# Mamba-2 scan and merged experts on one core: an earlier decay store, another load order, and new constants for the planner

## The chip, the cores and the metric

The kernel runs on one core of a Trainium2 chip. The core has five engines that run side by side, each in the order of its own instructions: TensorE (PE, with its weight loads shown as PEld), VectorE (DVE), ScalarE (ACT), GpSimd (POOL) and SyncE (SP). SP computes nothing here; it issues nearly all DMA transfers, in order. The metric is device time in microseconds, the median of several runs. Lower is better.

## The reference, cut to what matters

Two blocks follow each other. The first is a Mamba-2 scan over 4 sequences of 768 positions, with 8 heads of width 32 and a state of 16. The reference works in chunks; within a chunk:

```python
cum = np.cumsum(la, axis=-1)                    # la = log of the clipped decays a
L = np.exp(cum[:, :, :, None] - cum[:, :, None, :]) * causal
M = np.einsum('bhin,bhjn->bhij', Cc, Bc) * L
y = M @ xc + (Cc @ state) * np.exp(cum)[..., None]
state = decay_full * state + sum_j(Bc_j xc_j * decay_from_j)
```

The result, 3,072 tokens of width 256, goes through four experts, each with a hidden width of 1,024:

```python
p = domain_probs / (domain_probs.sum(-1, keepdims=True) + 1e-09)
for e in range(E):
    out += p[:, e:e + 1] * (np.maximum(x @ w1[e], 0.0) @ w2[e])
```

All of it is float32.

## The kernel before, in words

**The scan.** The sequences are cut into 24 chunks of 128 positions. The matrix L of a chunk is not made with exponentials: DVE runs a multiply-add scan over the decays (`scan`, L494), with the first decay of each head set to zero. For chunks 0 to 2 the decays are spread over the partitions by matmuls (`spread`, L618) and scanned from PSUM. From chunk 3 on (`SPREAD = 3`) they come by DMA: the cut decays `a_cut` are stored once to DRAM (`acut_d`), and `load_decays` (L438) reads a chunk's 4 KB back into all 128 partitions, 512 KB in all, into a tile `ab`. An uncut copy goes to `ac_d`; `load_heads` (L444) reads it for chunks from 4 on, and a scan at L778 makes the state's decays `dec` of it. `score` (L477) makes C times B, DVE multiplies it with L (L796, the masks `MT`), and `outputs` (L818, L510) makes a chunk's results.

**The experts.** The hidden width of an expert is cut into 4 slices of 256, so there are 16 slices. Five blocks of tokens are worked on (`ORDER = B, B, B, H, H`); a block B takes four chunks, a block H six. Within a block the products of slices and token pairs are done with fewer block products than the plain way, in the manner of Strassen: sums of weight blocks (L961), sums of token blocks (L980) and sums of results take the place of some products. A product is four matmul records at L872. A first-layer product is gated, which is ReLU times the probability, on DVE (L907); sums of gated values (L899) feed the second layer. Its products are collected by "houses", pairs of accumulators in one PSUM bank: ACT seeds the bank from an SBUF copy (L886), PE adds the terms, ACT copies it back (L1127). The tuple `B.houses` is the order in which a block B visits them. Second-layer products of one unit are interleaved one to one with first-layer products of the next (`put(behind, seq)`). A unit of block B has two pairs of slices, so each number of a house stands for two products. Sums of weights that a later block needs again are stored to DRAM (`w_d`, L966) and loaded back.

**What sets the order.** The first 13 us are written out by hand, from the loads at L535 to the store at L697: there stand `store_decays(0)`, the loads of first-layer weights 2 and 3, tokens 3, decays 3 and second-layer weights 0 and 1 after it, and `store_decays(1)` (`ac_d`) at the end. Both stores are issued by ACT (L596), the loads by SP. All the rest is ordered by a planner, `Plan.run`, when the program is built. PE's order is given. For the other engines it keeps a clock for each engine and starts, of what can start, the operation with the earliest latest time. A transfer goes through 8 lanes and a modelled bus (`RATE`, KB per us); `self.bus` is when the bus is free. An operation that reads loaded data can start `MARGIN` us after the modelled landing, and so can one that takes a buffer over from a transfer, unless SP issues it. `NEAR` and `WORTH` let DVE stand idle for a short time when something clearly more urgent is about to be ready. An operation that DVE or POOL may do goes to POOL only if it ends there before its latest time and DVE has enough to do. The planner's times are not waited for on the chip: only the order within each engine comes out of it, and semaphores do the rest.

Of the kernel before, what the change touches and what calls it, by code (L numbers as in the profile page):

```python
# [24 lines left out]
EARLY = 1, 2, 3, 4, 5, 6, 7, 8, 9, 10  # L25
SOFT = 1
ROUND = 0, 3, 2, 0, 4
RATE, MARGIN = 330.0, 2.0
AFTER = 1
HOLD = 12.0  # L30
NEAR, WORTH = .0, 1.0
WAIT = .15
LANES, ISSUE = 8, .48
HELD = ("x", "w"), (5, 8), (0, 7)
LAST = (0, 1), (0, 2), (1, 1), (1, 2), (0, 0), (1, 0)
LATE = (13, 2), (6, 9), (11, 4), (10, 12), (3,), (1, 14), ("x", "w"), (5, 8), (0, 7)
# [8 lines left out]

class Home:
    def __init__(self, tile_):
        self.tile, self.free, self.full, self.dma = tile_, 0.0, False, False


class Value:
    def __init__(self, kind, seeded=False, fills=True):
        self.kind, self.seeded, self.fills = kind, seeded, fills
        self.home, self.writers, self.readers, self.left, self.end = None, [], [], 0, 0.0
        self.keeps = None

    @property
    def t(self):
# [12 lines left out]
class Plan:  # L71
# [20 lines left out]
    def add(self, on, fn, reads=(), writes=(), part=(), lag=None, due=None, reuse=None, two=False,  # L92
            port=True, after=None, kb=0, hold=0.0, pieces=1):
        w = Work(on, fn, (.16 if "PE" in on else .09) if lag is None else lag)
        w.hold = hold
        w.two, w.port, w.after, w.kb, w.pieces = two, port, after, kb, pieces
        w.due, w.reuse = due, reuse
        w.ready = 0.0
        for v in reads:
            w.needs.update(v.writers)  # L100
            w.ready = max(w.ready, getattr(v, "ready", 0.0))
            v.readers.append(w)
        for v in writes:
            w.needs.update(v.writers)
            w.needs.update(v.readers)
            v.writers, v.readers = [w], []
        for v in part:
            w.needs.update(v.readers)
            v.writers = v.writers + [w]
        w.needs.discard(w)  # L110
        keeps = [v.keeps for v in (*reads, *writes, *part) if v.keeps]
        for v in dict.fromkeys([*reads, *writes, *part, *keeps]):
            w.touched.append(v)
            v.left += 1
        for n in w.needs:
            n.feeds.append(w)
        self.all.append(w)
        return w

# [3 lines left out]
    def times(self, line, at):  # L123
        t = at
        for w in line:
            w.nominal = t
            t += w.on["PE"]
        self.ws = {}
        for w in reversed(self.all):
            us = min(w.on.values()) + w.lag  # L130
            last = [f.latest - WAIT for f in w.feeds]
            if "PE" in w.on:
                last.append(w.nominal + us)
            elif not last:
                last.append(t if w.due is None else w.due().nominal)
            if w.hold:
                last += [n.nominal + w.hold for n in w.needs if "PE" in n.on]
            w.latest = min(last) - us
            for v in w.touched:
                if v.kind == "W" and v.home is None:  # L140
                    v.latest = min(w.latest, getattr(v, "latest", w.latest))
                    self.ws[v] = None
        return t
# [41 lines left out]
    def run(self, line, at, begin):  # L185
# [14 lines left out]
                    waiting[e].append(w)  # L200
        done, todo, head = [], len(self.all), 0
        stuck = 0
        self.stall, self.port, self.bus = [], 0.0, 0.0
        self.lanes = [begin["SP"] + .4 * i for i in range(LANES)]
        while todo:
            e = min(t, key=lambda e: t[e])
            now = t[e]
            best, soon, near = None, None, None
            late = self.late = max(0.0, t["PE"] - line[head].nominal) if head < len(line) else 0.0
            for w in waiting[e]:  # L210
                if w.start is not None or e == "PE" and w.place != head:
                    continue
                ready = max([w.ready, w.after.nominal + late if w.after else 0.0] + [
                    n.end + (MARGIN if n.kb and e != "SP" else -n.lag if n.by == e == "PE" else HOP)
                    for n in w.needs])
                if len(w.on) > 1 and e == "POOL":
                    if max(ready, now) + w.on[e] > w.latest + late + SLACK or self.backlog(
                            waiting["DVE"], now, t["DVE"], w) < BACK:
                        continue
                rank = w.latest  # L220
                if e == "DVE" and w.two and self.port > now + 0.05:
                    rank += YIELD
                if best is not None and ready <= now and rank >= best[0]:
                    continue
                when, homes = self.homed(
                    w, max(now, ready, self.port if e == "POOL" and w.port else 0.0))
                if when is None:
                    continue
                if when <= now + 0.02:
                    if best is None or rank < best[0]:  # L230
                        if e == "DVE" and w.two:
                            when = max(when, self.port)
                        best = rank, w, when, homes
                else:
                    if e == "DVE" and when <= now + NEAR and (near is None or rank < near[0]):
                        near = rank, when
                    if soon is None or when < soon:
                        soon = when
# [16 lines left out]
            _, w, when, homes = best  # L255
# [13 lines left out]
                head += 1  # L269
                self.stall.append((when, when - now, w))  # L270
            for v, h in homes.items():
                v.home = h
                if h in self.spare[v.kind]:
                    self.spare[v.kind].remove(h)
            for v in w.touched:
# [45 lines left out]
B = Scheme()  # L321
# [4 lines left out]
B.tokens = ((5, (0, 1), (0, 0), -1), (6, (1, 1), 5, -1), (7, (1, 1), (0, 1), -1), (4, (1, 0), 6, -1))  # L326
B.right = {1: (0, 0), 2: (1, 0), 3: (1, 1)}
B.shared = {1: ((6, 7), (5, 3)), 2: ((7, 5), (6, 3))}
B.houses = ((1, 7), (5, 6), (3, "x"), (2, 4))
B.plain = {(0, 0): 2, (1, 0): 4, (0, 1): 3, (1, 1): "x"}  # L330
ORDER = B, B, B, H, H

# [8 lines left out]
def kernel(  # L341
# [10 lines left out]
    nc = tc.nc  # L352

    NCH, _, W = xbc.shape
# [36 lines left out]
    acut_d = tc.dram_tile([NCH, NH, P], FP32, name="acut_d")  # L391
    ac_d = tc.dram_tile([NCH, NH, P], FP32, name="ac_d")
# [10 lines left out]
    def some(n, shape, name, pool=const):  # L403
        return [pool.tile(shape, FP32, name=f"{name}{i}") for i in range(n)]

    homes = {
        "V": some(NV, [P, 2, FB], "v"),
        "W": some(NW, [P, 2 * FB], "w"),
        "bank": some(8, [P, 512], "bank", psum),
        "xb": some(4, [P, W], "xb"),  # L410
        "ab": some(2, [P, NH * P], "ab"),
        "ah": some(3, [HN, P], "ah"),
        "LT": some(1, [P, 2, NH, P], "LT"),
        "MT": some(2, [P, 2, NH, P + N], "MT"),
# [13 lines left out]
    def load_tokens(c, xb):  # L428
        src = xbc[real(c)]
        if len(turned(c)) > 1:  # L430
            nc.sync.dma_start(out=xb[:, :OBT], in_=src[:, :OBT])
            for there, here, n in turned(c):
                nc.sync.dma_start(out=xb[here:here + n, OBT:], in_=src[there:there + n, OBT:])
        else:
            nc.sync.dma_start(out=xb, in_=src)

    def load_decays(c, ab):
        nc.sync.dma_start(  # L438
            out=ab, in_=acut_d[real(c)].rearrange("h s -> (h s)").partition_broadcast(P))
# [10 lines left out]
    def load_w1(fb, w):  # L450
        e, f = divmod(fb, EPB)
        nc.sync.dma_start(
            out=w.rearrange("p (a f) -> p a f", a=2),
            in_=w1[e].rearrange("(a p) f -> p a f", a=2)[:, :, f * FB:f * FB + FB])

    def load_w2(fb, w):
        e, f = divmod(fb, EPB)
        nc.sync.dma_start(
            out=w.rearrange("p (j m) -> p j m", j=JJ),
            in_=w2[e, f * FB:f * FB + FB].rearrange("(j p) m -> p j m", p=P))  # L460
# [69 lines left out]
    a_sb = const.tile([NCH * NH // 2, 2, P], FP32, name="a_sb")  # L530
# [11 lines left out]
    xb = homes["xb"]  # L542
# [47 lines left out]
    a_cut = const.tile([NCH * NH // 2, 2, P], FP32, name="a_cut")  # L590
    nc.gpsimd.tensor_copy(a_cut, a_sb)
    nc.gpsimd.memset(a_cut[:, :, 0:1], 0.0)

    def store_decays(kind):
        d, sb = ((acut_d, a_cut), (ac_d, a_sb))[kind]
        nc.scalar.dma_start(  # L596
            out=d.rearrange("c h s -> (c h) s").rearrange("(p r) s -> p r s", r=2), in_=sb)

    BANK = homes["bank"]
    rows = NCH * E  # L600
# [58 lines left out]
    scan_quarters(0, LT[0], four, 1)  # L659
    fade(0, MT[0], xb[0], LT[0])  # L660
    mask(1, ctm[1], xb[1])
    store_decays(0)
    for fb in range(2, 4):
        load_w1(fb, homes["W"][fb])
    load_tokens(3, xb[3])
    load_decays(3, homes["ab"][0])
    for fb in range(2):
        load_w2(fb, homes["W"][4 + fb])
    spread(1, four)
    for r in (2, 3):  # L670
        masked(0, r, MT[0], LT[0], seven[r], 0)
# [22 lines left out]
        keep_state(1, A[1][:, t], y[:, P:])  # L694
    mask(2, ctm[0], xb[2])
    nc.sync.dma_start(out=p_d.rearrange("e c s -> c e s"), in_=p_sb)
    store_decays(1)  # L697

# [691 lines left out]
    for i, w in enumerate(leave_last(len(blocks) - 1, O, LAST)):  # L1392
# [1 line left out]
    line.extend(behind)  # L1394

    done = plan.run(line, now, {"PE": now, "DVE": now - .6, "ACT": now + 1.0, "POOL": now - 2.0,
                                "SP": now + .4})
    for w in done:
        w.fn(w.by)

# [44 lines left out]
```

## Time and profile before

| | us |
|---|---|
| median of 3 runs | 634.73 (634.13 to 636.03) |
| profiled execution | 636.64 |
| its span, first to last instruction | 634.9 |
| PE busy | 623.9 (98%) |
| DVE busy | 518.2 (82%) |
| ACT, POOL busy | 267.2, 231.0 |
| DMA, mean rate over the span | 198 GB/s |
| granted TensorE clock, mean | 0.994 |

The span leaves out what lies around the first and the last instruction, so the profiled execution's time is 1.74 us longer. An engine's busy time is a share of the span; PE's share is so high that only its gaps and its clock can be shortened by another order. A line of waits gives the engine and line that waited, what released it, and then the total, the number of waits and the longest. In the timeline, idle time before a group stands in brackets with what ended it.

### The profile page before, as it was taken

The numbers are of one execution on the slowest core, as the hardware profiler recorded it, in microseconds if no ns is written. First come the engines' busy times: TensorE is split into PE (matmuls) and PEld (weight loads), VectorE is DVE, ScalarE is ACT, GpSimd is POOL, SyncE is SP. The second block draws the span as 40 slices with busy tenths as digits, with TensorE's granted clock in tenths as the row PEclk, the third lists the DMA queues.
The fourth block names the chain that finished last, engine by engine and source line by source line (L and its number), as shares of the span: only waits on it lengthen the run. The fifth ranks groups of instructions, "written<-read, shape, count | busy, mean of one in ns | idle before, by whom it ended". The sixth has DMA issues, their size and how long they took to land.

```text
span 634.9 us, 10315 instructions
## 1 busy us (share of the span) xinstructions
PE 623.9 (98%) x3443; PEld 531.0 (84%) x3443; DVE 518.2 (82%) x823; ACT 267.2 (42%) x563; POOL 231.0 (36%) x256
## 2 busy tenths in 40 slices
PE   9897999999999999999999999999999999999997
PEld 5686888788888888888888888888888888888886
DVE  6698889899679698857978989859796968779684
ACT  4231265333355343435534334455435245454541
POOL 4143546745246465464462603130031420112020
PEclk9999899999999999999999999999999999999999
DMA  5999578754799966699999627546222229643001
GB/s 169 291 325 299 192 255 251 258 175 119 241 341 303 319 201 193 183 308 333 328 304 340 228 35 269 150 131 189 85 75 82 61 40 343 204 137 124 1 1 50
DMA packets 111732, 125.87 MB, mean 198 GB/s; under 512 B 28852, under 2 KB 78272, under 8 KB 111680
## 3 DMA queue, kind: packets, MB, share of 16 engines
q1 hardware_dynamic: 111300, 124.97, 61.6%
q8 instruction: 27, 0.44, 0.3%
q10 hardware_dynamic: 380, 0.25, 0.1%
q14 instruction: 25, 0.20, 0.1%
HBM read 100.30 MB, written 24.89 MB: 197 GB/s over the span
## 4 chain that ended last, share of the span: by engine, by line
PE 92%; DVE 3%; DMA 3%; issue 1%; SPq 0%; ACT 0%; DVEq 0%; ACTq 0%
PE bank L872 86%; PE bank L477 2%; PE bank L510 2%; DMA acut_d<-a_cut 1%; DMA ab<-acut_d 1%; DMA ah<-ac_d 1%; DVE LT L494 1%; PE bank L642 1%; DVE v L899 1%; PE bank L818 1%; DVE v L907 1%; DVE w L961 0%; DMA w_d<-w 0%; DVE dec L778 0%; PE bank L1250 0%
## 5 line engine op out<-in xcount | busy, mean ns | idle before, releaser
L872 PE MATMUL bank<-v,w 128*128 128x256 f32 x1864 | 441.6, 382 | 3.6 <-DVE v L907 3.3
L872 PEld LDWEIGHTS bank<-v,w 128*128 128x128 f32 x1864 | 353.7, 191 | 58.1 <-issue 4.9
L872 PE MATMUL bank<-Y,w 128*128 128x256 f32 x792 | 203.2, 379 | 0.5 <-ACT bank L886 0.5
L899 DVE TENSOR_TENSOR v<-v,v 128x512 f32<-128x512 f32 x219 | 174.9, 826 | 22.9 <-ACT v L881 20.2
L872 PEld LDWEIGHTS bank<-Y,w 128*128 128x128 f32 x792 | 150.2, 190 | 21.9 <-ACT bank L886 0.9
L907 DVE SCALAR_TENSOR_TENSOR v<-bank,gate 128x512 f32<-128x512 f32 x172 | 116.7, 682 | 43.7 <-PE bank L872 38.6
L899 POOL TENSOR_TENSOR v<-v,v 128x512 f32<-128x512 f32 x51 | 73.3, 1440 | 192.7 <-DVE v L907 121.7
L886 ACT COPY bank<-v 128x512 f32<-128x512 f32 (+1 forms) x192 | 108.7, 576 | 75.1 <-DVE v L899 48.2
L961 POOL TENSOR_TENSOR w<-w,w 128x256 f32<-128x256 f32 x106 | 92.6, 894 | 76.7 <-PE bank L872 48.9
L881 ACT COPY v<-bank 128x512 f32<-128x512 f32 x106 | 61.8, 584 | 112.4 <-PE bank L872 106.0
L1127 ACT COPY v<-bank 128x512 f32<-128x512 f32 x107 | 62.5, 585 | 109.5 <-PE bank L872 109.2
L494 DVE TENSOR_TENSOR_SCAN LT<-ab,ident 128x512 f32<-128x512 f32 x42 | 53.1, 1278 | 3.1 <-DMA ab<-acut_d 3.1
L899 DVE TENSOR_TENSOR v<-bank,v 128x512 f32<-128x512 f32 x40 | 27.4, 684 | 7.4 <-PE bank L872 6.8
L796 DVE TENSOR_TENSOR MT<-bank,LT 128x512 f32<-128x512 f32 (+1 forms) x48 | 28.4, 633 | 0.7 <-PE bank L477 0.7
L961 POOL TENSOR_TENSOR w<-w 128x256 f32<-128x256 f32 x14 | 12.5, 896 | 41.6 <-DMA w<-in_w_dram 32.4
L504 POOL TENSOR_TENSOR MT<-xb,LT 128x64 f32<-128x64 f32 (+1 forms) x28 | 14.2, 516 | 33.6 <-DVE LT L494 33.4
L470 ACT ACTIVATE ctm<-xb,tmask 128x128 f32<-128x128 f32 x48 | 16.2, 393 | 23.2 <-DMA xb<-in_xbc_dram 23.0
L1178 POOL TENSOR_TENSOR v<-v,v 128x256 f32<-128x256 f32 x16 | 15.2, 968 | 27.4 <-DVE v L1178 19.8
L1032 DVE TENSOR_TENSOR bank<-bank,v 128x512 f32<-128x512 f32 x22 | 15.2, 689 | 7.1 <-PE bank L872 7.1
L1178 DVE TENSOR_TENSOR v<-v,v 128x256 f32<-128x256 f32 x44 | 17.4, 429 | 3.4 <-ACT v L1127 3.2
L781 POOL TENSOR_TENSOR cts<-ctm,dec 128x256 f32<-128x256 f32 x20 | 17.4, 886 | 4.3 <-DVE dec L778 3.3
L961 DVE TENSOR_TENSOR w<-w,w 128x256 f32<-128x256 f32 x32 | 16.5, 525 | 1.3 <-DMA w<-in_w_dram 0.8
(72 smaller groups left out, 212.4 us busy)
## 6 DMA issues: line engine op xcount, KB each, us to landing
w<-in_w_dram SPq DMA_DIRECT2D x130, 256.0 KB
w<-w_d SPq DMA_DIRECT2D x130, 256.0 KB
w_d<-w SPq DMA_DIRECT2D x82, 256.0 KB
ab<-acut_d SPq DMA_DIRECT2D x21, 512.0 KB
w<-in_w_dram SPq DMA_DIRECT2D x38, 128.0 KB
gate<-p_d SPq DMA_DIRECT2D x10, 384.0 KB
xb<-in_xbc_dram SPq DMA_DIRECT2D x17, 192.0 KB
gate<-p_d SPq DMA_DIRECT2D x11, 256.0 KB
```

Of the source, the lines that this page charges most:

```text
L470: nc.scalar.mul(ctm[:, t], xb[:, OCT:OCT + P], tmask[:, t:t + 1])
L494: nc.vector.tensor_tensor_scan(out=LT.rearrange("p h s -> p (h s)")[:, lo:lo + w], data0=src, data1=ident.rearrange("p h s -> p (h s)")[:, ...
L781: plan.add({"POOL": .72}, lambda e: nc.gpsimd.tensor_mul(s["cts"].t, s["ctm"].t, s["dec"].t.unsqueeze(1).to_broadcast([HN, NT, P])), reads ...
L796: nc.vector.tensor_mul(s["MT"].t[:, js, h, 0:P], g, s["LT"].t[:, js, h])
L872: nc.tensor.matmul(out=o, lhsT=w[:, j], rhs=x if half is None else x[:, j], start=(start and j == 0), stop=(j == 1), skip_group_check=True)
L881: act(.5, lambda e: nc.scalar.copy(out=flat(v), in_=bank.t), reads=[bank], writes=[v])
L886: act(.54 if to > FB else .32, lambda e: nc.scalar.copy(out=bank.t[:, :to], in_=flat(v)[:, :to]), reads=[v], writes=[bank])
L899: plan.add(engines, lambda e: (on(e).tensor_add if sign > 0 else on(e).tensor_sub)(flat(v), whole(x), whole(y)), reads=[x, y], writes=[v], ...
L907: dve(D512, lambda e: nc.vector.scalar_tensor_tensor(out=h.t, in0=whole(x).rearrange("p (j m) -> p j m", j=JJ), scalar=0.0, in1=g.t[:, 2 * ...
L961: plan.add({"POOL": .72} if due else B256, lambda e, r=r, x=x, y=y, sign=sign: (on(e).tensor_add if sign > 0 else on(e).tensor_sub)(view(r ...
L1127: act(.5, lambda e: nc.scalar.copy(out=flat(v), in_=bank.t), reads=[bank], writes=[v])
L1178: plan.add(engines, lambda e: (on(e).tensor_add if sign > 0 else on(e).tensor_sub)(o[1](), x[1](), y[1]()), reads=[v for v in vs if v is n ...
```

## The change

The edit does five things.

1. The store of the cut decays (`acut_d`) moves from ACT's queue to SP's, and in the program from after the mask of chunk 1 to right after the data is made. On SP's queue it stands behind the load of tokens 2. The store of `ac_d` stays on ACT, where it was.
2. The loads that followed it move up with it, in another order: first-layer weights 2 and 3 and tokens 3 as before, then second-layer weights 0 and 1, then the decays of chunk 3. Before, the decays came ahead of the second-layer weights.
3. Constants of the planner: `MARGIN` 2 to 4 us; the bus begins 4 us later than SP; lanes begin .5 us apart, not .4; SP begins at 14.2, not 13.6; `NEAR` .3 us, not 0, but only before 25 us (`FIRST`).
4. `B.houses` is (1, 7), (3, "x"), (5, 6), (2, 4), where (5, 6) stood second.
5. New fields and a table `URGENT`, which is empty, so that they change no order.

```diff
-RATE, MARGIN = 330.0, 2.0
+RATE, MARGIN = 330.0, 4.0
-NEAR, WORTH = .0, 1.0
+NEAR, WORTH, FIRST = .3, 1.0, 25.0
+URGENT = {}
...
-            w.latest = min(last) - us
+            w.latest = min(last) - us - URGENT.get(w.number, 0.0)
...
-        self.stall, self.port, self.bus = [], 0.0, 0.0
-        self.lanes = [begin["SP"] + .4 * i for i in range(LANES)]
+        self.stall, self.port, self.bus = [], 0.0, begin["SP"] + 4
+        self.lanes = [begin["SP"] + .5 * i for i in range(LANES)]
...
-                    if e == "DVE" and when <= now + NEAR and (near is None or rank < near[0]):
+                    if e == "DVE" and when <= now + NEAR and now < FIRST and (near is None or rank < near[0]):
...
-B.houses = ((1, 7), (5, 6), (3, "x"), (2, 4))
+B.houses = ((1, 7), (3, "x"), (5, 6), (2, 4))
...
-    def store_decays(kind):
-        d, sb = ((acut_d, a_cut), (ac_d, a_sb))[kind]
-        nc.scalar.dma_start(
+    def store_decays(engine, d, sb):
+        engine.dma_start(
             out=d.rearrange("c h s -> (c h) s").rearrange("(p r) s -> p r s", r=2), in_=sb)
+
+    store_decays(nc.sync, acut_d, a_cut)
+    for fb in range(2, 4):
+        load_w1(fb, homes["W"][fb])
+    load_tokens(3, xb[3])
+    for fb in range(2):
+        load_w2(fb, homes["W"][4 + fb])
+    load_decays(3, homes["ab"][0])
...
     mask(1, ctm[1], xb[1])
-    store_decays(0)
-    for fb in range(2, 4):
-        load_w1(fb, homes["W"][fb])
-    load_tokens(3, xb[3])
-    load_decays(3, homes["ab"][0])
-    for fb in range(2):
-        load_w2(fb, homes["W"][4 + fb])
...
-    store_decays(1)
+    store_decays(nc.scalar, ac_d, a_sb)
...
-                                "SP": now + .4})
+                                "SP": now + 1.0})
```

## The prediction, made before the result was known

> **What bounds the kernel now.** I read the page first. TensorE is the bound:
>
> ```profile
> span 634.9 us, 10315 instructions
> ...
> PE 623.9 (98%) x3443; PEld 531.0 (84%) x3443; DVE 518.2 (82%) x823; ACT 267.2 (42%) x563; POOL 231.0 (36%) x256
> ```
>
> So the edit can act only on the 11.0 us in which PE is idle, and on any time in which PE is busy but slow. The view of waits, cut to PE, says where the inner idle time is:
>
> ```profile
> PE bank L872 <- DVE v L907: 3.3, 1, 3.3
> PE bank L510 <- DVE MT L796: 1.9, 2, 1.7
> ...
> PE bank L872 <- ACT bank L886: 0.5, 1, 0.5
> ...
> PE bank L872 <- DVE v L899: 0.3, 1, 0.3
> ```
>
> Two waits matter, one of 1.70 us and one of 3.33 us. The chain that ended last gives their causes, in order of time (start, length, what):
>
> ```profile
> 7.37 6.96 DMA acut_d<-a_cut
> ...
> 14.35 6.36 DMA ab<-acut_d
> ...
> 20.80 2.34 DVE LT L494 x2
> ...
> 55.22 5.53 DMA ah<-ac_d
> ...
> 60.84 0.14 DVE dec L778
> ...
> 61.90 5.55 PE bank L872 x12
> ```
>
> The first: ACT's store of the cut decays lands 6.96 us after its issue, SP's broadcast load of chunk 3's decays waits for it and lands 6.36 us later, the scans follow, and PE's outputs of chunk 3 start at 24.87 instead of 23.17. The second is on DVE's timeline:
>
> ```profile
> 57.34 1.26 DVE L907 SCALAR_TENSOR_TENSOR v<-bank,gate 128x512 f32<-128x512 f32 x2
> 60.84 0.42 DVE L778 TENSOR_TENSOR_SCAN dec<-ah,zeros 128x128 f32<-128x128 f32 x1 [2.24 <-DMA ah<-ac_d]
> 61.18 0.67 DVE L907 SCALAR_TENSOR_TENSOR v<-bank,gate 128x512 f32<-128x512 f32 x1
> ```
>
> DVE runs in order. It stands 2.24 us at a decay scan whose heads have not landed, and the gate behind it, which PE needs, is late. Windows of 1 us (window, length, then busy time of PE, PEld, DVE, ACT and POOL, clock, DMA share, GB/s) show a second bill:
>
> ```profile
> 60.00:61.00 1.00, 0.00 (x0) 0.00 (x0) 0.16 (x1) 0.00 (x0) 0.00 (x0) 0.92 0.91 283
> 61.00:62.00 1.00, 0.10 (x1) 0.10 (x1) 1.00 (x3) 0.00 (x0) 0.00 (x0) 0.50 0.97 305
> ...
> 66.00:67.00 1.00, 1.00 (x4) 0.64 (x2) 1.00 (x3) 0.00 (x0) 0.84 (x2) 0.50 0.91 328
> 67.00:68.00 1.00, 1.00 (x10) 0.60 (x12) 1.00 (x2) 0.00 (x0) 1.00 (x1) 0.66 0.94 316
> ```
>
> After the wait PE runs at half clock. Its 12 matmuls take 5.55 us; at the late row's rate (924 in 199.63 us, 0.216 each) they would take 2.59, so 2.96 us go there. The second wait costs 3.33 + 2.96 = 6.29 us.
>
> **What the Trainium skill says.** TensorE: Matmul & The Clock Gate, in its section on the HAM clock gate, says that an idle window of about 3.4 us halves the clock and a busy one restores it, on a window that runs freely. The trace agrees in kind: half clock from about 60.9 to 67.5, two such windows, after 3.33 us without matmuls; the wait of 1.70 us left the clock at 1.00. DMA: Bandwidth & Descriptors, Issuing engines are not separate DMA queues, says that all queues run on the same 16 engines, so SP instead of ACT saves issue time alone. Its section on queues, rings and completion order says that a completion lands only after all earlier writes of that DMA engine, across queues. The trace agrees: 96 KB took 6.96 us while over 1 MB was still moving. Perfetto Trace Analysis, in the part on HWDGE DMA, says that the wait stands in the issuing sequencer; here SP issues nothing from 7.43 to 14.35.
>
> **The store and the loads behind it.** Its source is ready here:
>
> ```profile
> 6.19 0.10 POOL L592 MEMSET a_cut<- 96x2 f32 x1
> ```
>
> SP is free at 5.79 (xb 2 issued), so the store goes at about 6.34, 1.03 us before ACT's 7.37. Issue times, from the rows of before: store 0.34, two first-layer weights 0.94, tokens 3 0.61, two second-layer weights 0.98: SP reaches the decays' load at about 9.3 with gaps. The first-layer weights and tokens 3 go about 0.9 us later than before; PE wants those weights at 19.45, and ACT's mask of tokens 3 (14.89) comes before scores at 18.80, so I cost that at nothing. ACT loses a 0.34 us issue beside running copies: nothing.
>
> When does the store land? Ahead of it stand the loads up to xb 2: 4 + 128 + 96 + 128 + 384 + 512 + 320 KB, with 56 KB of ACT's, 1,628 KB. The windows of 3 us moved 19, 238, 238 and 297 GB/s, that is 57, 771, 1,485 and 2,376 KB by 3, 6, 9 and 12 us. With its own 96 KB the store's bytes are through at 9.0 + 239/297 = 9.8. In before the bytes were through at about 13 and it landed at 14.33, some 1.4 us more: 11.2. Bounds: 9.8, and 6.34 + 6.96 = 13.3.
>
> The decays' load goes then at 11.2, not 14.35. Ahead of it are 3,068 KB in all, of which 2,140 have moved: 930 KB, or 3.1 us, which before were not there (the second-layer weights now lie in front, not behind). Its own 512 KB take 1.7 and a landing 1.3: 17.3. The upper bound keeps the whole 6.36 us behind the 3.1: 20.7, no gain at all. I take 18.2, nearer the low end since 1.5 MB that shared the old 6.36 us are partly gone. From landing to PE's start were 24.87 - 20.74 = 4.13 us (two scans, a gate, three masks), so PE waits for nothing if it lands by 19.04. Gain 1.70, slack 0.8; what is late next is PE itself.
>
> A side effect: DMA moved only 81 GB/s from 12 to 15, because SP stood. That hole, up to 0.65 MB or 2 us, gets filled, and the queue is saturated from 25 to 58 (313 to 332 GB/s), so the loads there come up to 2 us sooner, against a PE that is 1.70 sooner.
>
> **The planner.** It emits every instruction after 13.2 us, so the orders on DVE, POOL and SP change all over; which orders come out cannot be read from the trace. The margin after a landing grows from 2 to 4, the bus starts 4 us busy, SP starts 0.6 us later, lanes are 0.1 us further apart. All say the same: take loads to be later. Where DVE stood 2.24 us at the scan, 2 us and more of added delay in the plan put the gate (0.67 us, ready since its bank's matmuls ended near 58.5) in front. Then PE's 3.33 us go, and the clock stays up: 6.29. Bounds: if only the landing moves, by 2 us against PE's 1.70, the wait shrinks by 0.3 and the clock still drops, so +0.3; and below nothing, since a weight sum put 2 us later can miss its product: that is the slow rival. The short idle allowed to DVE (0.3 us, before 25 us) is worth at most a gate early: nothing. The unused tables cost nothing.
>
> **The other house order.** House (3) moves ahead of (5, 6). Each term is 4 matmuls of 0.216, 0.863 us, interleaved one to one with first-layer ones: (3) has two terms, so sums 5 and 6 get 4 x 0.863 = 3.45 us more, and 3 is a plain gate output that exists before 7 does. That covers DVE's late sums (the 0.28 us wait on L899). Against it, the shared weights (7, 5) stay 3.45 us longer. I count 0 and keep 0.3 for the range.
>
> **Sum.** 1.70 + 3.33 + 2.96 = 7.99. I take off 0.6 by choice for short waits of a new order (before has 0.18, 0.54 and 0.28 of that kind): 7.4. Span 634.9 to 627.5; the profiled execution, 1.74 more than its span, 636.64 to 629.2; the median of the runs shown is 634.73, so 627.3.
>
> **The rivals.** First, only the early wait goes and the one near 58 us stays with its half clock, since the order there survives or another DMA-fed operation stands in the same place: 1.70 + 0.3 to 1.0, so 632.0 to 632.7. For it: DMA is saturated there and four head loads lie behind a weight load that waits for its buffer at 54.27. Against: three separate terms push those scans back.
>
> Second, nothing moves: decays land at 20.7 and the planner moves the wait elsewhere at the same price: 634.
>
> Third, slower. Place: the first shared-weight unit, whose weight sums DVE makes from 28.9 to 45.4 for products from 44.37 on, where DVE is busy 9.59 and 9.34 of 10 us. A margin of 4 ranks those sums behind gates that wait for PE, and POOL takes fewer (it takes one only if it ends before its latest time), so sums go to the fuller engine. Each PE wait of over 3 us costs about 6.3 with its clock. Two give 12.6 - 8.0 = +4.6: 639.3. It decides once new waits and clock drops exceed 8.0. For it: DVE's load; against: PE had no wait from 25 to 58.5, and DVE stood 2.56 us at 26 to 28.9 for a weight that now comes sooner.
>
> **How the numbers follow.** Chances: forecast 0.50 (own range 625.5 to 629.5), early wait only 0.23, nothing 0.06, slower 0.21. 0.3% (1.9 us) is about what a measurement here tells from no change. Faster: 0.50 and 0.20 of the first rival; same: its other 0.03 and 0.06; slower: 0.21. The range goes to 625.5 below (all short waits gone too, 634.73 - 8.99 = 625.74) and to 637.5 above, which leaves out about half of the slow case.
>
> **What would show it.** Right: the store issued near 6.3 and landed near 11, decays 3 landed by 19, no wait of PE before L510 at 23; clock 1.00 through 60 to 70; PE's waits on DVE under 2 us in sum. Wrong: decays' load landing after 20; a matmul group at half clock anywhere; new DVE waits of PE at 40 to 60 or 100 to 150.

## The result, and the profile after

The changed kernel takes 628.86 us (median of 4 runs, 628.72 to 629.06), the kernel before 635.38 (4 runs, 634.13 to 637.73) on the same chip: a ratio of 0.9893, 95% interval 0.9863 to 0.9924. That is 6.5 us or 1.1% less. In a second set it took 629.0 us (6 runs, 628.71 to 629.07) beside 635.77 (14 runs): 0.9900, interval 0.9883 to 0.9918. (In one of the experiments below, the first set of the start alone, two runs took 1,089 and 1,319 us, in the profiled one a matmul 0.68 us on the mean instead of 0.38; these two are left out.)

The page of the changed kernel, span and busy time:

```profile
span 626.9 us, 10322 instructions
...
PE 620.4 (99%) x3443; PEld 529.6 (84%) x3443; DVE 522.7 (83%) x822; ACT 267.6 (43%) x563; POOL 235.6 (38%) x257
```

The span is 8.0 us shorter. PE's idle time fell from 11.0 to 6.5 us, and its busy time by 3.5 us for the same 3,443 matmuls. Most of the second part is the clock: the prediction's sum had 2.96 us for the matmuls at half clock, and none are at half clock now. The view of waits, cut to PE, holds neither of the two waits of before:

```profile
PE bank L874 <- ACT bank L888: 0.7, 1, 0.7
PE bank L874 <- DVE v L901: 0.7, 1, 0.7
...
PE bank L874 <- DVE v L909: 0.3, 1, 0.3
```

The start, on SP's timeline (start, length, engine, line): the store goes at 6.33, and the load that waits for it at 10.65, not 14.35.

```profile
6.33 0.33 SPq L597 DMA_DIRECT2D acut_d<-a_cut  x1
...
10.65 0.34 SPq L440 DMA_DIRECT2D ab<-acut_d  x1
```

The place of the second wait, on DVE's timeline, and then the clock there in a window of 10 us, first before the change and then after it (the clock is the number before the DMA share):

```profile
58.34 1.28 DVE L909 SCALAR_TENSOR_TENSOR v<-bank,gate 128x512 f32<-128x512 f32 x2
...
61.34 1.49 DVE L780 TENSOR_TENSOR_SCAN dec<-ah,zeros 128x128 f32<-128x128 f32 x1
```

```profile
60.00:70.00 10.00, 8.10 (x35) 5.79 (x36) 7.74 (x15) 0.26 (x1) 4.57 (x5) 0.66 0.86 288
60.00:70.00 10.00, 10.00 (x48) 8.81 (x47) 10.00 (x17) 5.02 (x9) 5.43 (x5) 1.00 0.34 117
```

Gates stand in front of the scan, nothing waits for a load, and PE is busy at full clock through the window in which it ran at 0.66 before. By landmarks of PE, from its timeline and the chain that ended last: its outputs of chunk 3 start at 22.72 instead of 24.87 (2.15 us), the second scores after them at 58.49 instead of 67.39 (8.90), the scores at 171.12 come at 162.27 (8.85), and the last 924 matmuls at 418.35 instead of 426.26 (7.91). Nearly all of the gain is made by 60 us; some 0.9 is given back later, 0.67 of it in the wait on L901 at 301.

### The profile page after: what moved, and what is told of

It is laid out like the page before. It is cut to its first block, busy times and chain, and to the rows that moved or that the text cites. A ratio compares the mean times of both kernels' runs of the same rounds, so it can differ in the third digit from the quotient of the medians.

```text
span 626.9 us, 10322 instructions
## 1 busy us (share of the span) xinstructions
PE 620.4 (99%) x3443; PEld 529.6 (84%) x3443; DVE 522.7 (83%) x822; ACT 267.6 (43%) x563; POOL 235.6 (38%) x257
## 4 chain that ended last, share of the span: by engine, by line
PE 91%; DVE 7%; issue 1%; ACT 1%; DVEq 0%; ACTq 0%
PE bank L874 85%; PE bank L479 2%; PE bank L512 2%; DVE v L901 2%; DVE v L909 1%; DVE w L963 1%; DVE LT L496 1%; PE bank L651 1%; PE bank L820 1%; PE bank L627 1%; DVE dec L780 0%; DVE Y L982 0%; DVE MT L798 0%; PE bank L1252 0%; ACT A L522 0%
## 5 line engine op out<-in xcount | busy, mean ns | idle before, releaser
L901 DVE TENSOR_TENSOR v<-v,v 128x512 f32<-128x512 f32 x219 | 178.4, 844 | 21.0 <-ACT v L883 19.5
L901 POOL TENSOR_TENSOR v<-v,v 128x512 f32<-128x512 f32 x51 | 72.1, 1417 | 219.3 <-DVE v L909 124.1
L963 POOL TENSOR_TENSOR w<-w,w 128x256 f32<-128x256 f32 x106 | 96.9, 932 | 58.3 <-PE bank L874 35.0
L901 DVE TENSOR_TENSOR v<-bank,v 128x512 f32<-128x512 f32 x40 | 27.4, 685 | 9.6 <-PE bank L874 9.5
L1180 POOL TENSOR_TENSOR v<-v,v 128x256 f32<-128x256 f32 x18 | 17.2, 967 | 26.1 <-DVE v L1180 19.8
```

The costliest lines, as they stand in the source:

```text
L901: plan.add(engines, lambda e: (on(e).tensor_add if sign > 0 else on(e).tensor_sub)(flat(v), whole(x), whole(y)), reads=[x, y], writes=[v], ...
L963: plan.add({"POOL": .72} if due else B256, lambda e, r=r, x=x, y=y, sign=sign: (on(e).tensor_add if sign > 0 else on(e).tensor_sub)(view(r ...
L1180: plan.add(engines, lambda e: (on(e).tensor_add if sign > 0 else on(e).tensor_sub)(o[1](), x[1](), y[1]()), reads=[v for v in vs if v is n ...
```

## The experiments

The question was which part of the change brought the gain near 58 us. My theory had been the planner: it puts the decay scans behind the gates that they held. The rival: all loads there are late together, and starting them sooner is what counts.

**The start alone.** The kernel before with the new hand-written start; planner and house order as before.

```diff
+    store_decays(nc.sync, acut_d, a_cut)      # with the loads behind it, as in the change
...
-    store_decays(0)                           # and the loads behind it
```

> The kernel before with only the hand-written start changed: the store on SP, the loads moved up, second-layer weights in front of decays 3; planner and house order as before. Theory (two separate waits): the store goes at 6.3 and lands near 10.7, the wait of 1.70 us before the outputs of chunk 3 is gone, the order of DVE is as before, so DVE still stands at the decay scan near 57 to 61 us and PE still drops to half clock: gain 1.7 to 2.7 us. Rival (one cause: late loads): since the loads come up to 2 us sooner, the heads land in time too, and the gain is 5 to 8 us.

Measured: ratio 0.9925, interval 0.9900 to 0.9949. The median of its four other runs is 630.68 us beside 636.07, 5.4 us less; by the ratio it is 4.8. That is far above the 1.7 to 2.7 of my theory and at the lower end of the rival's 5 to 8. Run again for its profile:

> The kernel before with only the start of the change once more, for its profile. The theory now: the wait near 58 us is one of a queue of loaded operands that all came late, so loads that start sooner cure it as well as another order does. Then weights and heads land 2 to 3.5 us sooner against the kernel before, PE waits under 1.5 us in all from 55 to 62 and the clock stays at 1.00 there: 4 to 6 us faster. Rival (the gain is all at the start): PE waits over 2.5 us near 58 and drops its clock.

Measured: 630.7 us beside 635.33, ratio 0.9922 (0.9893 to 0.9951), 4.6 us. PE's timeline of it, waits in brackets:

```profile
56.73 1.13 PE L872 MATMUL bank<-v,w 128*128 128x256 f32 x4 [0.90 <-DVE v L907]
58.73 1.97 PE L872 MATMUL bank<-v,w 128*128 128x256 f32 x8 [0.87 <-DVE v L907]
...
69.27 4.55 PE L872 MATMUL bank<-v,w 128*128 128x256 f32 x20 [1.26 <-DVE MT L796]
```

The order of DVE is that of before, and DVE still stands at the same scan, but 1.34 us and only until 55.67, not 60.84. PE waits 1.77 us in two pieces, a little over the 1.5 that I had allowed, and the clock stays at 1.00. A further wait of 1.26 us at 69, behind masks, is one that the kernel before does not have. In the eight runs of this kernel, four of each set, the granted clock is 0.999 or 1.000. So the start alone takes away the half clock and nearly half of the second wait.

Why the loads come so much sooner shows in the first 30 us, first before the change and then with the new start (the last number is GB/s):

```profile
0.00:30.00 30.00, 27.00 (x187) 17.51 (x188) 19.80 (x52) 11.12 (x37) 8.58 (x25) 1.00 0.74 225
0.00:30.00 30.00, 28.70 (x198) 19.38 (x199) 24.79 (x60) 11.78 (x39) 10.41 (x27) 1.00 0.90 288
```

That is 6.75 and 8.64 MB. The 1.89 MB between them are, as an estimate at the 323 GB/s of before from 30 to 55 us, 5.9 us of transfers; the scan went 5.2 us sooner.

**The planner's constants alone.**

```diff
-RATE, MARGIN = 330.0, 2.0
+RATE, MARGIN = 330.0, 4.0
...
+        self.stall, self.port, self.bus = [], 0.0, begin["SP"] + 4
...
+                                "SP": now + 1.0})
```

The lanes and DVE's short idle went with it.

> The kernel before with only the planner's constants of the change (margin, idle allowed to DVE, bus, lanes, SP's start); start and house order as before. Theory: the scans move behind the gates, PE's wait near 58 us and its half clock are gone, the wait of 1.70 us stays: gain about 6.3 us, 5 to 6.5 with new short waits. Rival (the order needs the faster start as well): the planner's order, made for loads that come sooner, meets loads that come later, and DVE or PE stands elsewhere: gain under 3 us or a loss.

Measured: 629.91 us beside 636.07, ratio 0.9914 (0.9889 to 0.9939), 6.2 us. No wait of PE on DVE or ACT from 25 to 70 in its profile, clock 1.00 there. The planner alone cures it too, as the theory had it. The early wait, which I expected to stay at 1.70 us, is 0.29 us in this profile. The intervals of the two single cures overlap, so which of them is worth more is not shown.

**The two scans moved back.** One edit in the kernel before: after planning, the scans of chunks 9 and 10 get a place behind the two gates that followed them, and the head loads that take their tiles over go behind them.

```diff
     done = plan.run(...)
+    order = [w for w in done if w.by == "DVE"]
+    late = [st[c]["decw"] for c in (9, 10)]
+    gate = order[order.index(late[0]) + 4]
+    for i, w in enumerate(late):
...
+        w.start = gate.start + .001 * (i + 1)
...
+    done.sort(key=lambda w: w.start)
```

> The kernel before with one edit: on DVE the decay scans of chunks 9 and 10 go behind the two gates that followed them (and the loads that take over their tiles behind them). Theory (these scans held the gates, and the wait cooled the clock): PE's wait of 3.33 us and the 2.96 us at half clock go, gain 6.0 to 6.3 us, clock 1.00 from 60 to 70. Rival (DMA is saturated there, so another loaded operand is late in its place): gain under 3 us and a new wait of PE within 10 us. Rival (the clock drops without the wait): gain 3.3 us at most.

Measured: 636.25 us beside 636.07, ratio 1.0013 (1.0001 to 1.0026). No gain at all: the first rival holds. DVE's timeline, then PE's, then the two windows of 0.25 us in which the clock drops and comes back:

```profile
60.62 0.42 DVE L961 TENSOR_TENSOR w<-w,w 128x256 f32<-128x256 f32 x1 [3.04 <-DMA w<-in_w_dram]
```

```profile
61.79 3.13 PE L872 MATMUL bank<-v,w 128*128 128x256 f32 x8 [3.03 <-DVE v L907]
```

```profile
62.25:62.50 0.25, 0.25 (x2) 0.22 (x2) 0.25 (x2) 0.00 (x0) 0.00 (x0) 0.86 0.74 262
...
65.75:66.00 0.25, 0.25 (x8) 0.18 (x8) 0.25 (x1) 0.00 (x0) 0.25 (x1) 0.82 0.81 258
```

With the scans out of the way DVE stands at the next operation that reads a load, a weight sum, and the next gate is behind that one. The weight sum goes within 0.2 us of where the scan went. PE waits 3.03 us there, after 0.75 us a little earlier, and the half clock is back, for 3.4 us instead of 6.8. The scan was not the cause; it was the first of a row of operations whose loads were late.

**The start and the two scans.** Both edits together.

> The kernel before with the hand-written start of the change and the two scans moved back, planner and house order as before. Theory: both gains add, 1.7 to 2.7 and 6.0 to 6.3, so 7.7 to 9 us, at or below the changed kernel; then planner constants and house order brought nothing besides moving those scans. Rival (the wider reordering and the house order matter): less than 6 us.

Measured: 629.53 us, ratio 0.9910 (0.9886 to 0.9933), 6.5 us. This differs from the run before it in the start alone, with one order on DVE near 58, so it prices the sooner loads: the same weight sum goes at 57.10 instead of 60.62, 3.5 us sooner; PE waits 1.07 us where it had waited 0.75 and 3.03; the clock stays up; 6.7 us in the medians, 4.7 in the spans of the two profiles (632.3 and 627.6). In the first 30 us 7.4 and 8.7 MB were moved, by the same estimate a lead of 3.9 us. The two gains don't add up to the 7.7 to 9 that I expected.

**Single constants taken back from the changed kernel.** First the margin:

```diff
-RATE, MARGIN = 330.0, 4.0
+RATE, MARGIN = 330.0, 2.0
```

> The changed kernel with the margin after a landing at 2 us again. If the margin is what put the scans behind the gates: a wait of DVE on a load before a gate from 50 to 65, 1 to 3 us slower than the changed kernel (630 to 632). If start and busy bus do it: within 0.5 us of the changed kernel.

Measured: 627.96 us (626.97 to 628.13) beside 635.33, ratio 0.9876 (0.9852 to 0.9899). Then the bus, with lanes and SP's start:

```diff
-        self.stall, self.port, self.bus = [], 0.0, begin["SP"] + 4
+        self.stall, self.port, self.bus = [], 0.0, 0.0
```

> The changed kernel with the planner's queue idle at first again (bus, lanes and SP's start as before). If the busy bus matters: 1 to 3 us slower than the changed kernel. If the margin does it alone: within 0.5 us of it.

Measured: 627.9 us (627.11 to 628.04), ratio 0.9876 (0.9849 to 0.9902). Neither is needed beside the other. In both profiles DVE waits for loads under 1 us in all after the start, and the only wait of PE on DVE or ACT after 10 us is one of 0.95 us at 199 in the first and one of 0.40 us at 108 in the second.

All ten runs of these two lie below all ten of the changed kernel (628.71 to 629.07), by about 1 us in the medians. They ran on another chip than the second set of the changed kernel, where the kernel before measured 635.33 and 635.77; so the difference of 0.2% is likely, not certain. The changed kernel has 1.65 us of such waits and, in its second profile, 1.66, which fits. Both constants taken back:

> The changed kernel with margin 2 and the planner's queue idle at first together, so that start, house order and DVE's short idle are what is left of the change. Theory (either of the two constants is enough, but one is needed): DVE stands at a loaded operand near 55 to 62 again as with the start alone, 630 to 631.5. Rival (the start alone does the work and the house order the rest): within 0.7 us of the changed kernel.

Measured: 629.44 us (628.31 to 632.48), ratio 0.9906 (0.9885 to 0.9927), beside 629.0 of the changed kernel in the same set. The median is under what I expected and 0.4 us above the changed kernel, as the rival had it. But the runs reach 3.4 us above those of the changed kernel, and the profile, of the longest of them, shows why. DVE's timeline and a window of 4 us:

```profile
56.76 0.42 DVE L780 TENSOR_TENSOR_SCAN dec<-ah,zeros 128x128 f32<-128x128 f32 x1 [3.82 <-DMA ah<-ac_d]
```

```profile
60.00:64.00 4.00, 3.95 (x12) 2.79 (x16) 3.97 (x8) 0.59 (x1) 1.63 (x3) 0.50 0.96 348
```

The scan is back in front of the gate; PE waits 2.32 and 1.07 us and loses its clock. With the new start this order can still go wrong, by how the loads land. The other five runs left no profile, but their granted clock is on record: 1.000 in four of them and 0.997 in the one of 630.58 us. So most of them kept their clock.

**The house order taken back.**

```diff
-B.houses = ((1, 7), (3, "x"), (5, 6), (2, 4))
+B.houses = ((1, 7), (5, 6), (3, "x"), (2, 4))
```

> The changed kernel with the houses of block B in the old order. Theory (3.45 us more for sums 5 and 6): one more short wait of PE on DVE's sums in blocks of kind B, 0.3 to 1 us slower than the changed kernel. Rival: within 0.3 us, or faster, since the sums are ready anyway.

Measured: 628.45 us (628.09 to 629.19), ratio 0.9889 (0.9866 to 0.9912). No slower than the changed kernel. Its profile does have a wait of PE on a sum (0.95 us at 93, on L901), but it lacks others; the rival holds, and the house order is worth nothing that these runs can show.

**The queue of the store.** The changed kernel with the early store on ACT, at the same place of the program, run beside the changed kernel itself:

```diff
-    store_decays(nc.sync, acut_d, a_cut)
+    store_decays(nc.scalar, acut_d, a_cut)
```

> The changed kernel itself, on the chip of the next three, so that they can be set against it: 628.5 to 629.1, ratio near 0.989. If margin 2 or an idle bus alone is truly better than both together, it stays about 0.9 us above what those two measured (627.9).

> The changed kernel with the early store of the cut decays on ACT's queue at the same place of the program. If only the earlier place counts: the same time. If the queue counts: ACT stands at the store until POOL has made the data at 6.3, the mask of chunk 0 behind it (4.2 in the changed kernel) goes at about 6.7, PE's first scores move from 6.0 to about 7.5 and all behind them, 1 to 2 us slower than the changed kernel.

Measured: 629.0 us for the changed kernel, as expected. With the store on ACT 633.05 us beside it, ratio to the kernel before 0.9951 (0.9926 to 0.9976), so 4 us lost, twice what I expected. ACT's timeline, PE's, and a window of 4 us:

```profile
6.92 0.34 ACTq L597 DMA_DIRECT2D acut_d<-a_cut  x1
7.37 0.69 ACT L472 ACTIVATE ctm<-xb,tmask 128x128 f32<-128x128 f32 x2 [3.13 <-DMA xb<-in_xbc_dram]
```

```profile
8.12 1.24 PE L479 MATMUL bank<-ctm,xb 32*128 32x256 f32 x8 [2.34 <-ACT ctm L472]
```

```profile
8.00:12.00 4.00, 3.45 (x25) 1.91 (x25) 2.54 (x6) 1.56 (x6) 1.78 (x3) 0.50 0.86 277
```

The masks stood behind the store's wait for its data as foreseen. I had not foreseen that PE, without work for 2.34 us, would run the next microseconds at half clock. The nine runs fall in two groups by it: three with a granted clock of 0.999 took 630.07 to 630.32 us, 1.1 to 1.3 more than the changed kernel and as expected; the six with 0.991 to 0.994, the profiled one among them, took 632.19 to 634.66. The bracket of the masks names a load of tokens; those had landed by 4.22 in the changed kernel, and the store's wait is what stood before them.

**The order of the loads.** Decays 3 ahead of second-layer weights 0 and 1 again.

```diff
-    for fb in range(2):
-        load_w2(fb, homes["W"][4 + fb])
     load_decays(3, homes["ab"][0])
+    for fb in range(2):
+        load_w2(fb, homes["W"][4 + fb])
```

> The changed kernel with the load of decays 3 in front of the second-layer weights 0 and 1 again. By the prediction's sum the 1.5 MB in front delay the decays: they would land up to 2 us sooner here, but SP would stand from about 8.3 until the store lands at 10.7 and all later loads come 1 us later; PE waits in neither case, so within 0.5 us of the changed kernel. Rival (the order of these loads is what cures the wait near 58): 2 us slower or more.

Measured: 629.81 us (628.59 to 630.78) beside 629.0, ratio to before 0.9912 (0.9893 to 0.9931). About 0.8 us slower in the median; the spans differ by 0.5. SP issues those weights at 10.99 instead of 8.35. PE's waits differ in one place, the wait on L901 at 301: 0.95 us here, 0.67 in the changed kernel. A small gain of that part is likely; its path is not shown.

## Why the prediction was right, and where not

**The result.** 627.3 was forecast, 628.86 measured, inside the forecast's own range of 625.5 to 629.5. The span came to 626.9, not 627.5. Both waits and the half clock went, as the sum said; that the total came so near is in part luck, as the first wait and the cause show.

**The store.** Issue at 6.34 forecast, 6.33 measured; landing at 11.2 forecast, 10.65 measured.

**The decays behind the weights.** I had added 3.1 us for 930 KB in front and taken 18.2, with 17.3 as the low end. The scans went at 18.26 without a wait, right behind a gate, so the landing was earlier. ACT's store of `ac_d` went at 15.79 behind a wait that the trace gives to this load; if that is right, the landing was near 15.8, some 5.1 us after the issue, where it took 6.36 us before without these weights in front. Then the step "or 3.1 us, which before were not there" failed: the weights in front cost little or nothing. The slack was larger than I wrote, the conclusion the same.

**The first wait.** It went, but its 1.70 us were probably not the gain of a usual run. Three profiles have the start of before. Only one of them has that wait in full: with the planner's constants alone it is 0.29 us, and with only the scans moved it is missing. ACT's store goes behind ACT's copies of PE's first scores, at 7.37, 6.7 and 6.5 us in these three, and its data were there at 14.35, 13.79 and 11.75. On SP the store hangs on POOL alone: it goes at 6.26 to 6.50, and its data are there at 10.38 to 11.13, in the nine profiles with it there. My sum took one execution for the kernel. I noted that it lay 1.91 us above the median shown and moved that offset over to the changed kernel, where the profiled run lies at the median (628.72 beside 628.86). That is why the median fell 6.5 us where the spans fell 8.0.

**The second wait and the clock.** Both went, 6.29 us in the sum. That the clock was about half of it in the profiled execution is shown by PE's busy time, which fell by 3.5 us where the sum had 2.96. With the scans moved and the new start added it fell by 1.5 us (622.4 to 620.9), since the half clock lasted half as long there, and PE's idle time by 3.2. The loss was regular: 41 of the 42 runs of the kernel before that list a clock have 0.993 to 0.997, one 0.999; the ten of the changed kernel have 0.999 or 1.000.

**The cause.** Here a step failed. I gave the 6.29 to the planner, and priced the sooner loads at "the wait shrinks by 0.3 and the clock still drops, so +0.3". I let the loads there gain 2 us, the width of the hole in the transfers from 12 to 15 us, 0.65 MB. They gained 3.5 to 5.2, since with the new start the transfers were ahead by 1.3 to 1.9 MB at 30 us, and the start alone brought 4.6 to 5.4 us. The first rival, in which only the early wait goes (632.0 to 632.7), was priced by the same step; the start alone, at 630.7, lies below it. Also, the single scan in front of the gate, from which I argued, could be taken away without any gain. The right total came from two cures of one fault, each nearly enough: 4.6 to 5.4 us and 6.2 us alone, 6.5 to 6.8 together. I had named one of them and got the sum of both nearly right, which was luck.

**The margin.** "2 us and more of added delay in the plan put the gate in front" is right of the constants together, but not of the margin: with the busy bus it is not needed, and the other way round. DVE's short idle was not tried alone.

**The house order, and short waits.** House order at 0: borne out. The 0.6 us taken off for short waits: 1.65 and 1.66 us in the two profiles against 1.00 of before, so 0.65; a choice that happened to fit.

**The slow rival.** No wait of PE stands between 25 and 80 in the changed kernel. The weight sums were in time at this margin: DVE did 10.00 of 10 us in the window from 40 to 50, and PE still had its operands.

## What to carry to other kernels

When an in-order engine stands at an operation whose load is late, look at the next ones in its queue before blaming that one: if their loads are late too, moving it only moves the wait. Two cures for the same wait must not be added; try each alone. And when you price a long wait of TensorE, allow for the clock that may go with it: the 3.33 us before cost 2.96 more, and a wait that measured 2.34 us in the profile made two groups of runs, 1.9 to 4.6 us apart.

## What the runs showed of the hardware

Half clock followed PE waits of 3.33 us (before), 0.75 and 3.03 (scans moved), 2.32 and 1.07 (both constants back) and 2.34 alone (store on ACT). It did not follow 1.70 (before), 0.90, 0.87 and 1.26 (start alone) or 1.07 (start and scans). Worked out from windows of 0.25 us, it lasted 6.8 us in three of these profiles and 3.4 with the scans moved, so one length or twice that length. It began 2.3 us into the wait before the change, 2.1 us into the wait with the store on ACT, but 1.0 us (both constants back, ahead of the second wait) and 0.6 us (scans moved) after PE had gone back to work. So the prediction's words "after 3.33 us without matmuls" were not exact: the drop was at 60.85, when PE had been idle for 2.3.

The Trainium skill, TensorE: Matmul & The Clock Gate, gives in its section on the HAM clock gate an idle window of about 3.4 us, on a window that runs freely. The lengths of 3.4 and 6.8 us and the changing place of the drop fit such a window. That PE must idle through all of it does not fit: in the 3.4 us ahead of the four drops it had been idle for 2.1 to 2.8. Three of the nine runs with the store on ACT kept their clock; whether their wait was as long is not known, as they left no profile.

The spread of the runs changed with the kernel: 632.94 to 638.6 us over all runs of the kernel before, 628.71 to 629.07 over ten of the changed one. Two things fit this: a store that hangs on PE's first scores, which began at 6.53, 5.86 and 5.67 us in three profiles with the start of before, and a wait near the length at which the clock drops. Neither was measured for itself.
